# Linear attention and a gated MLP in one kernel: the output projection joined to the down products of two more token pairs, the gate and up products of three FF-tile pairs as seven products instead of eight, and three of four h sums moved to VectorE

## Chip, core and metric

One NeuronCore of one Trainium2 chip runs the whole program in one launch. The metric is the device time in microseconds (us). The kernel before took 211.93 us, the median of three runs (211.37 to 212.01). The execution that was profiled took 212.13 us.

## What is computed

The input x has 2048 tokens of 512 values. It is normalised once (xn), and two branches and the input itself are added.

```python
xn  = layernorm(x)
qkv = xn @ wqkv                              # 32 heads of 16
pq, pk = q @ w_phi, k @ w_phi                # per head
phi = concat(softmax(p), softmax(-p))        # of pq and of pk, 32 features
kv, z = phi_k^T v, sum(phi_k)                # over all tokens
o   = (phi_q kv) / (phi_q z + 1e-6)
out = x + o @ wo + ((xn @ w_gate) * (xn @ w_up)) @ w_down    # F = 1792
```

## The kernel before

**Tiles.** Tokens come in 16 tiles of 128, or 8 pairs of tiles p = 0 to 7. F is cut into 14 FF tiles of 128, taken as 7 pairs (tile ft with tile ft + 7). The model dimension of 512 is four blocks of 128.

**Who does what.** TensorE (PE) does all products into PSUM. ScalarE (ACT) takes exponentials and copies gate products (and snapshots of partial sums) out of PSUM. VectorE (DVE) multiplies gate by up into the array h (`hT`), adds the pieces of the seven-product schemes, sums the softmax denominators and divides. GpSimd (POOL) forms sums of weights and of h in SBUF. The queue of SyncE (SP) issues loads, transposing DMAs and stores.

**Seven products.** A 2 by 2 block product normally takes 8 block products. The kernel does many of them in Winograd's form with 7, which need sums of blocks made beforehand on either side, and additions behind. For the tokens 512 to 1535, and 6 of the 7 FF-tile pairs, gate and up are done so (`BLOCK`, with `WSUMS` for the weights on GpSimd and `XSUMS` for the tokens on VectorE). The down product of each token pair is done so too: `SSUMS(p)` makes four sums S3, S1, S2, S4 of h (128 by 896 float16 each) on GpSimd, `TSUMS` the sums of the weights, and the steps P1 to P7 do seven matmuls of 256 columns each.

**The output projection.** `CAT_STEPS(p)`, for the pairs in `CAT` (1 to 5), also puts the attention output through the same seven products: each P step gets two more matmuls (P1o to P7o), with sums `SOSUMS(p)` of the attention output and `TOSUMS` of wo on GpSimd. `DOWN_STEPS(p)`, for pairs 0, 6 and 7, adds wo in the plain way: 16 matmuls of 256 columns, four of them in the step W22.

**The last 512 tokens.** `U2(ft, s_lo)` does gate and up for one FF tile and 256 tokens: 8 matmuls of 256 columns, one ScalarE copy (`ge`) and one VectorE product (`h`). 28 such units are spread between the down steps by `some(fr)`, with `Q(t)` (query features) and `NUM(t)` (attention numerator, VectorE steps nd, nr, no).

**Order.** The program records steps in the order of the source; `_plan` then reorders them on each engine by its own costs, dependencies and priorities, and `_emit_all` writes each engine's list with semaphore waits. Each engine then runs its list strictly in that order: an instruction that waits holds up all behind it. A PSUM bank is reused in the order of recording, from a ring of banks; the down steps use two fixed banks. In `sums`, a sum placed on VectorE is marked `lock`, so that the planner lets it run only while GpSimd does nothing.

```python
e3, e1, e2, e4 = (DVE if c == "D" else POOL for c in SE.get(p, "PPPP"))
sums(e3, S3, A11, A21, ALU.subtract, f"S3.{p}", 0)
sums(e1, S1, A21, A22, ALU.add, f"S1.{p}", 0)
sums(e2, S2, S1, A11, ALU.subtract, f"S2.{p}", 0)
sums(e4, S4, A12, S2, ALU.subtract, f"S4.{p}", 0)
```

The helper lines that the profile names: L510 is every matmul but the warm-up, L463 every ScalarE operation, L781 every sum of blocks (S, So, To, Ts, weight sums, and the X sums on VectorE), L731 and L729 the feature scaling on GpSimd, L940 the product h of `U2`, L1071 the additions (`post`) behind the down products, L862 and L868 those of `BLOCK`, L722 the softmax sums, L999, L1001 and L1005 the division.

Of the kernel before, what the change touches and what calls it, by code (L numbers as in the profile page):

```python
# [16 lines left out]
D = 512  # L17
# [342 lines left out]
PD = -1  # L360
PX = -1
SE = {}
UE = 1.6
QP0 = 1
QP1 = 2
# [2 lines left out]
TRQ = 1500.0  # L368
TRO = 800.0
PS = -1  # L370
CAT = (1, 2, 3, 4, 5)
SOE = POOL
TOE = POOL
PLN = 0
# [12 lines left out]
def _build(nc, es, A_x, A_wqkv, A_w_phi, A_wo, B_w_gate, B_w_up, B_w_down, out):  # L387
# [65 lines left out]
    def bank(b, lo=0, n=512):  # L453
        return psum[:, b * 512 + lo: b * 512 + lo + n]
# [67 lines left out]
    def group(o, pairs):  # L522
        n = len(pairs)
        return [(o, l, r, i == 0, i == n - 1) for i, (l, r) in enumerate(pairs)]
# [15 lines left out]
    def xnT(q, s_lo, n):  # L540
        return xnT_v[:, q, s_lo:s_lo + n]
# [328 lines left out]
    def BLOCK(kind, ft, ba):  # L870
# [58 lines left out]
                act_op(gslot(ft, 2), pa, name=f"ge{ft}.2", prio=PA)  # L929
        return [p1, p7, p6, p2, p4, p5, p3]  # L930

    def U2(ft, s_lo):
        b = nb()
        mm(group(bank(b, 0, 256), [(wg_v[:, q, ft * 128:(ft + 1) * 128], xnT(q, s_lo, 256)) for q in range(NQ)])
           + group(bank(b, 256, 256), [(wu_v[:, q, ft * 128:(ft + 1) * 128], xnT(q, s_lo, 256)) for q in range(NQ)]),
           name=f"gu{ft}.{s_lo}")
        g = gring()[:, 0:256]
        act_op(g, bank(b, 0, 256), name=f"ge{ft}.{s_lo}")
        h = hT_v[:, ft, hs(s_lo):hs(s_lo) + 256]
        dve(lambda e: e.tensor_tensor(out=h, in0=bank(b, 256, 256), in1=g, op=ALU.mult), [bank(b, 256, 256), g], [h],  # L940
            name=f"h{ft}.{s_lo}")

    def GU2(fts, s_lo, bg, bu, order):
# [48 lines left out]
    def NUM(t):  # L992
        nv = numb()
        mm([(nv[:, c, 0:68], qT_v[:, t % NQT, c, :], kvbd_v[:, c, :], True, True) for c in range(8)], name=f"n{t}")
        sm = qsum_v[:, t % 5, :].rearrange("p (c h s) -> p c h s", c=8, s=2)[:, :, :, 0]
        w = qw_v[:, t % 4, :]
        wv4 = w.rearrange("p (c h) -> p c h", c=8)
        den = nv[:, :, 64:68]
        dve(lambda e: e.scalar_tensor_tensor(out=wv4, in0=sm, scalar=1e-6, in1=den, op0=ALU.mult, op1=ALU.add),  # L999
            [qsum_v[:, t % 5, :], den], [w], cost=210.0, name=f"nd{t}")  # L1000
        dve(lambda e: e.reciprocal(out=w, in_=w), [w], [w], cost=360.0, name=f"nr{t}")  # L1001
        o = oslot(t)
        ov = o.rearrange("p (c h d) -> p c h d", c=8, h=4)
        src = nv[:, :, 0:64].rearrange("p c (h d) -> p c h d", h=4)
        dve(lambda e: e.tensor_tensor(out=ov, in0=src, in1=wv4[:, :, :, None].to_broadcast([128, 8, 4, 16]),  # L1005
                                      op=ALU.mult), [src, w], [o], cost=600.0, name=f"no{t}")
        dst = oT_v[:, t % 4, :, :]
        sc.dma(SP, dst, o, 131072, turn=True, reads=[o], writes=[dst], name=f"oT{t}").reserve = TRO
# [17 lines left out]
    def hA(half, t):  # L1026
        s = hs(t * 128)
        return hT_v[:, half * HF:(half + 1) * HF, s:s + 128]

    def SSUMS(p):  # L1030
        assert ui[0] >= (10 if p < 2 else NA2 if p < 6 else NA2 + (14, 28)[p - 6])
        S1, S2, S3, S4 = (S_v[:, p % 2, w] for w in range(4))
        A11, A12, A21, A22 = hA(0, 2 * p), hA(1, 2 * p), hA(0, 2 * p + 1), hA(1, 2 * p + 1)
        e3, e1, e2, e4 = (DVE if c == "D" else POOL for c in SE.get(p, "PPPP"))
        sums(e3, S3, A11, A21, ALU.subtract, f"S3.{p}", 0)
        sums(e1, S1, A21, A22, ALU.add, f"S1.{p}", 0)
        sums(e2, S2, S1, A11, ALU.subtract, f"S2.{p}", 0)
        sums(e4, S4, A12, S2, ALU.subtract, f"S4.{p}", 0)

    To_v = sbv("x", 12 * 512, 4 * 512).bitcast(F16).rearrange("p (w k j) -> p w k j", w=4, k=2)  # L1040
    So_v = sbv("vext", 0, 2 * 4 * 256).bitcast(F16).rearrange("p (r w k s) -> p r w k s", r=2, w=4, k=2)
# [37 lines left out]
    def DOWN_STEPS(p):  # L1079
# [1 line left out]
        final = p == NT // 2 - 1  # L1081
        S1, S2, S3, S4 = (S_v[:, p % 2, w] for w in range(4))
        A11, A12, A22 = hA(0, t1), hA(1, t1), hA(1, t2)
        pa, pb = bank(4, 0, 256), bank(5, 0, 256)
        t11, t21, t22 = (tf_v[:, p % 2, w] for w in range(3))

        def o(t, c):
# [31 lines left out]
                store(t1, 256, 256)  # L1119

        def s7():
            d = bank(nb(), 0, 256) if final else pb
            mm(prod(d, A12, B21, True) + wo_part(d, t1, 0), name=f"P2.{p}")
            post(p, o(t1, 0), d, t11, "c11")
            store(t1, 0, 256 if p == NT // 2 - 1 else 512)
# [18 lines left out]
    def CAT_STEPS(p):  # L1144
# [2 lines left out]
        S1, S2, S3, S4 = (S_v[:, p % 2, w] for w in range(4))  # L1147
        O1, O2, O3, O4 = (So_v[:, p % 2, w] for w in range(4))
        R1, R2, R3, R4 = (To_v[:, w] for w in range(4))
        A11, A12, A22 = hA(0, t1), hA(1, t1), hA(1, t2)  # L1150
        pa, pb = bank(4, 0, 256), bank(5, 0, 256)
        t11, t21, t22 = (tf_v[:, p % 2, w] for w in range(3))

        def o(t, c):
# [2 lines left out]
        def x(t, c):  # L1157
            return x_res(t)[:, c * 256:(c + 1) * 256]
# [4 lines left out]

        def s1():
            P(1, pa, A11, B11, oA(0, t1), oB(0, 0), True, False)
            post(p, t11, pa, x(t1, 0), "t11")

        def s2():
            P(2, pb, A12, B21, oA(1, t1), oB(1, 0), True, True)
            post(p, o(t1, 0), pb, t11, "c11")  # L1170

        def s3():
            P(7, pb, S3, T3, O3, R3, True, False)
# [15 lines left out]
        def s7():  # L1189
            P(3, pa, S4, B22, O4, oB(1, 1), False, True)  # L1190
            post(p, o(t1, 1), pa, x(t1, 1), "c12")
            store(t1, 0, 512)
        return [s1, s2, s3, s4, s5, s6, s7, lambda: None]

    one = nc.const_aps.tensor(1.0, [128, 512], BF16)

# [48 lines left out]
    rest = [(U, f, sg) for ft in range(NB, NF // 2) for f in (ft, ft + NF // 2) for sg in (1, 2)]  # L1245
    units += rest
    NA2 = len(units)
    units += [(U2, ft, s_lo) for s_lo in (1536, 1792) for ft in range(NF)]
    ui = [0]

    def nextU():
        if ui[0] < len(units):
# [44 lines left out]
    assert ui[0] >= NA  # L1297
    load_x(SP, 4, 4, name="rx")
    load_x(SP, 8, 4, name="rx")
    down = DOWN_STEPS(0)  # L1300
    nextU()
    KVS(NT, 1)
    KVX()
    ring_banks[0] = [0, 1, 2, 3]
    rp[0] = 0
    nextU()
    down[0]()
    down[1]()
    NUM(0)
    nextU()  # L1310
    SSUMS(1)
    nextU()
    NUM(1)
    TOSUMS(TOE)
    u0 = ui[0]
    n_left = len(units) - u0
    NP = NT // 2
    for p in range(NP):
        def some(fr):
            k = int(round(u0 + n_left * min(1.0, (p + fr) / (NP - UE))))  # L1320
            while ui[0] < min(k, len(units)):
                nextU()
        a, b = 2 * p + 2, 2 * p + QA
        if p == 2:
            load_x(SP, 12, 4, name="rx", slot=0)
        def Qs(pos):
            for k, at in ((0, QP0), (1, QP1)):
                if at == pos and b + k < NT:
                    Q(b + k)
        if p > 0:  # L1330
            down = CAT_STEPS(p) if p in CAT else DOWN_STEPS(p)
            Qs(0)
            down[0]()
            some(0.1)
            Qs(1)
            down[1]()
        some(0.2)
        if a < NT:
            NUM(a)
        if p == 0:  # L1340
            Qs(0)
            Qs(1)
        Qs(2)
        down[2]()
        some(0.4)
        Qs(3)
        down[3]()
        if 2 <= p + 1 < NP:
            SSUMS(p + 1)
        if a + 1 < NT:  # L1350
            NUM(a + 1)
            if p + 1 in CAT:
                SOSUMS(p + 1, SOE)
        some(0.5)
        down[4]()
        some(0.65)
        Qs(5)
        down[5]()
        some(0.8)
        down[6]()  # L1360
        some(1.0)
        down[7]()

    assert ui[0] == len(units)
    sc.chain("P6.7 P2.7 P5.7 P4.7 P3.7")

    for st in sc.steps:
        if st.eng in (ACT, DVE, POOL) and not isinstance(st.lane, tuple) and st.idx > late[0]:
# [40 lines left out]
```

The softmax here doesn't subtract the row's maximum and nothing guards it: scores larger than these inputs give would overflow.

## Time and profile before

| | |
|---|---|
| median of three runs | 211.93 us |
| profiled execution, whole | 212.13 us |
| its span, first to last instruction | 209.8 us |
| PE busy | 204.5 us (97%), 1603 matmul records; 1620 weight loads |
| VectorE busy | 158.7 us (76%), 307 instructions |
| ScalarE busy | 113.3 us (54%), 293 instructions |
| GpSimd busy | 169.6 us (81%), 215 instructions |
| granted TensorE clock | 1.00 |

Busy is the time in which an engine has at least one instruction under way; on VectorE and ScalarE the records of neighbours overlap by some 0.1 us. A few matmul records are missing, no weight load is. In the view by windows, each row gives the length of the stretch and then, for PE, PEld (weight loads), DVE, ACT and POOL, the busy time with the number of instructions in brackets. In rows of the timeline the first number is the start in us from the span's start, the second the length. A row of the groups ends in busy us, mean ns of one, and the idle time of the engine before them.

### The profile page before, as it was taken

What the parts mean: (1) busy time and instruction counts of PE and PEld (TensorE: products, weight loads), DVE (VectorE), ACT (ScalarE), POOL (GpSimd) and SP (SyncE); (2) the same over time, 40 slices, a digit from 0 to 9 for tenths busy, and PEclk for the clock granted to TensorE, in tenths of its full rate; (3) what the DMA queues carried; (4) which work ended last, traced back from release to release, by engine and by line L of the source; (5) the groups of instructions that cost most, each with busy time, mean ns of one, the idle gap of its engine ahead of it and who ended that gap; (6) DMA issues with size and microseconds to landing.
All of it is one profiled execution on the core that took longest, in us unless ns stands there. A gap on an engine that the chain in (4) does not pass through costs nothing.

```text
span 209.8 us, 4274 instructions
## 1 busy us (share of the span) xinstructions
PE 204.5 (97%) x1603; PEld 136.3 (65%) x1620; DVE 158.7 (76%) x307; ACT 113.3 (54%) x293; POOL 169.6 (81%) x215
## 2 busy tenths in 40 slices
PE   8999999999999999999999999999999999999995
PEld 3875444444454444454456797988978888799884
DVE  4857799998966797989987875948659486695743
ACT  4756999698796959697822613416144251531000
POOL 4061698439999999999999999999999989990540
PEclk9999999999999999999999999999999999999999
DMA  5999924964100000222521135183351705635211
GB/s 161 334 264 355 245 59 96 327 137 140 32 18 0 3 0 0 50 52 53 197 54 28 25 78 125 34 174 101 70 129 25 175 13 115 80 75 128 50 52 50
DMA packets 50244, 21.52 MB, mean 103 GB/s; under 512 B 37424, under 2 KB 50224, under 8 KB 50224
## 3 DMA queue, kind: packets, MB, share of 16 engines
q1 hardware_dynamic: 49552, 20.93, 40.5%
q10 hardware_dynamic: 672, 0.33, 0.6%
q8 instruction: 12, 0.20, 0.4%
q14 instruction: 8, 0.07, 0.1%
HBM read 10.24 MB, written 2.10 MB: 59 GB/s over the span
## 4 chain that ended last, share of the span: by engine, by line
PE 80%; POOL 7%; ACT 5%; DMA 3%; DVE 2%; issue 1%; DVEq 0%
PE ps L510 78%; ACT arena L463 5%; POOL arena L781 4%; DMA arena<-arena 3%; PE ps L1199 2%; POOL arena L731 2%; POOL arena L636 1%; DVE arena L781 1%; DVE arena L722 1%; POOL arena L729 0%; DVE arena L756 0%; ACT ps L463 0%; DVE arena L940 0%; DVE arena L1071 0%; DVEq L349 0%
## 5 line engine op out<-in xcount | busy, mean ns | idle before, releaser
L510 PE MATMUL ps<-arena 128*128 128x256 bf16 (+5 forms) x1593 | 200.3, 286 | 1.9 <-ACT ps L463 0.4
L510 PEld LDWEIGHTS ps<-arena 128*128 128x128 bf16 (+1 forms) x1610 | 135.0, 98 | 67.8 <-ACT arena L463 2.0
L781 POOL TENSOR_TENSOR arena<-arena 128x256 f16<-128x256 bf16 (+3 forms) x120 | 124.3, 1060 | 12.9 <-DVE arena L940 7.4
L463 ACT ACTIVATE arena<-ps 128x512 bf16<-128x512 f32 (+3 forms) x168 | 83.4, 533 | 67.9 <-PE ps L510 64.7
L722 DVE TENSOR_REDUCE arena<-arena 128x64 f32<-128x1024 bf16 x32 | 38.6, 1208 | 1.0 <-ACT arena L463 0.9
L1071 DVE TENSOR_TENSOR arena<-ps,arena 128x256 bf16<-128x256 f32 (+1 forms) x56 | 23.3, 422 | 17.4 <-PE ps L510 16.1
L463 ACT ACTIVATE arena<-arena 128x64 f32<-128x64 f32 (+4 forms) x96 | 28.4, 314 | 12.2 <-DVE arena L722 8.8
L731 POOL TENSOR_TENSOR arena<-arena 128x512 bf16<-128x512 bf16 x32 | 33.8, 1060 | 0.4
L940 DVE TENSOR_TENSOR arena<-ps,arena 128x256 f16<-128x256 f32 x30 | 12.4, 420 | 11.3 <-ACT arena L463 9.7
L862 DVE TENSOR_TENSOR arena<-ps,arena 128x512 f16<-128x512 f32 x24 | 16.1, 683 | 1.0 <-PE ps L510 0.8
L811 DVE TENSOR_TENSOR arena<-ps,arena 128x512 f16<-128x512 f32 x14 | 9.5, 684 | 4.9 <-PE ps L510 3.5
L756 DVE TENSOR_TENSOR arena<-ps,arena 128x512 bf16<-128x512 f32 x16 | 10.8, 683 | 2.1 <-ACT arena L463 1.5
L627 DVE BATCH_NORM_STATS2 arena<-arena 128x6 f32<-128x512 bf16 x16 | 10.5, 673 | 2.1 <-DMA arena<-in_A_x_dram 2.0
L868 DVE TENSOR_TENSOR ps<-ps,arena 128x512 f32<-128x512 f32 x12 | 8.2, 696 | 4.3 <-PE ps L510 3.0
L1005 DVE TENSOR_TENSOR arena<-ps,arena 128x512 bf16<-128x512 f32 x16 | 11.0, 685 | 0.3
L729 POOL TENSOR_TENSOR arena<-arena 128x32 f32<-128x32 f32 x32 | 8.3, 262 | 3.5 <-ACT arena L463 3.4
L609 POOL TENSOR_TENSOR arena<-arena 128x128 bf16<-128x128 bf16 x4 | 1.6, 428 | 8.7 <-DMA arena<-in_A_w_phi_dram 8.7
L636 POOL TENSOR_SCALAR arena<-arena 128x1 f32<-128x1 f32 x12 | 3.3, 290 | 6.0 <-ACT arena L463 6.0
L868 DVE TENSOR_TENSOR arena<-ps,arena 128x512 bf16<-128x512 f32 x12 | 8.0, 680 | 0.0
L463 ACT ACTIVATE ps<-ps 128x512 f32<-128x512 f32 x12 | 7.2, 600 | 0.0
L1001 DVE RECIPROCAL arena<-arena 128x32 f32<-128x32 f32 x16 | 5.6, 352 | 0.5
L1199 PE MATMUL ps<-const-bfloat16-1.0 128*128 128x512 bf16 x10 | 4.4, 626 | 0.8 <-PEq L1394 0.8
(22 smaller groups left out, 26.6 us busy)
## 6 DMA issues: line engine op xcount, KB each, us to landing
arena<-in_A_x_dram SPq DMA_DIRECT2D x6, 512.0 KB, 5.2
arena<-in_B_w_down_dram SPq DMA_DIRECT2D x1, 1792.0 KB, 7.6
out_dram<-arena SPq DMA_DIRECT2D x14, 128.0 KB, 2.0
arena<-in_B_w_gate_dram SPq DMA_DIRECT2D x1, 768.0 KB, 7.9
arena<-in_B_w_up_dram SPq DMA_DIRECT2D x1, 768.0 KB, 8.4
arena<-arena SPq DMA_TRANSPOSE x44, 2.5
arena<-in_B_w_gate_dram SPq DMA_DIRECT2D x2, 256.0 KB, 4.4
arena<-in_B_w_gate_dram SPq DMA_DIRECT2D x1, 512.0 KB, 6.1
```

Source lines behind the costliest of these rows:

```text
L463: return e.activation(out=out_ap, in_=in_ap, func=func, scale=scale, **kw)
L510: ins = e.matmul(o, lhsT=l, rhs=r, start=s, stop=p, skip_group_check=True)
L627: dve(lambda e, t=t: e.bn_stats(stats_v[:, t, :], x_tile(t)), [x_tile(t)], [stats_v[:, t, :]], cost=600.0, name=f"st{t}", win=win, prio=prio)
L722: dve(lambda e, ei=ei, so=so: e.tensor_reduce(out=so, in_=ei.rearrange("p (h f) -> p h f", f=16), axis=AX.X, op=ALU.add), [ei], [so], cost ...
L731: pool(lambda e: e.tensor_tensor(out=ev[:, :, 1, :], in0=ev[:, :, 1, :], in1=ratio[:, :, None].to_broadcast([128, H, 16]), op=ALU.mult), [ ...
L756: dve(lambda e: e.tensor_tensor(out=o1, in0=src, in1=rp_[:, :, :, None].to_broadcast([128, 8, 4, 16]), op=ALU.mult), [src, rs_v[:, t % 4, ...
L781: fn = lambda e: e.tensor_tensor(out=out_, in0=a_, in1=b_, op=op)
L862: dve(lambda e: e.tensor_tensor(out=h, in0=src, in1=g, op=ALU.mult), [src, g], [h], name=f"h{ft}.{sg}", prio=PD)
L868: dve(lambda e: e.tensor_tensor(out=o, in0=src, in1=sn, op=ALU.add), [src, sn], [o], name=name, prio=PD)
L940: dve(lambda e: e.tensor_tensor(out=h, in0=bank(b, 256, 256), in1=g, op=ALU.mult), [bank(b, 256, 256), g], [h], name=f"h{ft}.{s_lo}")
L1005: dve(lambda e: e.tensor_tensor(out=ov, in0=src, in1=wv4[:, :, :, None].to_broadcast([128, 8, 4, 16]), op=ALU.mult), [src, w], [o], cost=6 ...
L1071: dve(lambda e: e.tensor_tensor(out=out_, in0=in_ps, in1=in_sb, op=ALU.add), [in_ps, in_sb], [out_], cost=328.0, name=f"{name}.{p}")
```

## The change

Three things are changed in the program, and the planner makes a new order from it.

- `CAT` becomes (0, 1, 2, 3, 4, 5, 6): pairs 0 and 6 use `CAT_STEPS`, with `SOSUMS` on GpSimd for both.
- For FF-tile pairs 0, 1 and 2 (`NX = 3`) and the last 512 tokens, 12 of the 28 units `U2` are replaced by six `ZBLOCK`s (gate and up of each pair), each of 7 products of two matmuls of 256 columns. `ZXSUMS` (four sums of 128 by 512) and six `ZWSUMS` (four sums of 128 by 256 each) are recorded on GpSimd. Each `ZBLOCK` takes three of the four ring banks.
- `SED = 'PDDD'`: of the four h sums of each pair, S3 stays on GpSimd, and S1, S2 and S4 go to VectorE.

Also: the last pair's two fixed banks become 2 and 3, `U2` swaps the halves of its bank for the last tokens, and units are paced by a weight. The other new constants are left at values that change nothing.

```diff
-CAT = (1, 2, 3, 4, 5)
+CAT = (0, 1, 2, 3, 4, 5, 6)
+SED = 'PDDD'
+AB = {7: (2, 3)}
+NX = 3
+WSE = POOL
+XSE = POOL
...
+    def ZXSUMS():
+        X1, X2, X3, X4 = (Tz_v[:, w] for w in range(4))
+        for n, (o_, a_, b_) in enumerate(((X1, zB(0, 1), zB(0, 0)), (X3, zB(1, 1), zB(0, 1)), (X2, zB(1, 1), X1),
+                                          (X4, zB(1, 0), X2))):
+            sums(XSE, o_, a_, b_, ALU.subtract, f"Xz{n}", 0)
...
+        sums(WSE, S3, A(0, 0), A(1, 0), ALU.subtract, f"{kind}z3.{ft}", 0)
+        sums(WSE, S1, A(1, 0), A(1, 1), ALU.add, f"{kind}z1.{ft}", 0)
+        sums(WSE, S2, S1, A(0, 0), ALU.subtract, f"{kind}z2.{ft}", 0)
+        sums(WSE, S4, A(0, 1), S2, ALU.subtract, f"{kind}z4.{ft}", 0)
...
+    def ZBLOCK(kind, ft):
...
+        def p1():
+            pa = take("a")
+            xprod(pa, A(0, 0), zB(0, 0), True, "b1" + nm)
+            seed(take("c"), pa, "sd" + nm)
+        def p7():
+            pb = take("b")
+            xprod(pb, S(2), X3, True, "b7" + nm)
+            st["p7"] = zsnap()
+            act_op(st["p7"], pb, name="s7" + nm, prio=PB)
+        def p2():
+            xprod(st["c"], A(0, 1), zB(1, 0), False, "b2" + nm)
+            done(ft, 0, st["c"])
+            free("c")
+        def p6():
+            xprod(st["a"], S(1), X2, False, "b6" + nm)
+            st["u2"] = zsnap()
+            act_op(st["u2"], st["a"], name="s2" + nm, prio=PB)
+        def p4():
+            pb = st["b"]
+            xprod(pb, A(1, 1), X4, False, "b4" + nm)
+            if kind == "g":
+                zadd(zgslot(ft2, 0), pb, st["u2"], "a4")
+            else:
+                zadd(pb, pb, st["u2"], "a4")
+                done(ft2, 0, pb)
+            free("b")
+        def p5():
+            xprod(st["a"], S(0), X1, False, "b5" + nm)
+            if kind == "g":
+                zadd(zgslot(ft2, 1), st["a"], st["p7"], "a5")
+            else:
+                pt = bank(nb(), 0, 256)
+                zadd(pt, st["a"], st["p7"], "a5")
+                done(ft2, 1, pt)
+        def p3():
+            xprod(st["a"], S(3), zB(1, 1), False, "b3" + nm)
+            done(ft, 1, st["a"])
+            free("a")
+        return [p1, p7, p2, p6, p4, p5, p3]
...
-        e3, e1, e2, e4 = (DVE if c == "D" else POOL for c in SE.get(p, "PPPP"))
...
+        es = [DVE if c == "D" else POOL for c in SE.get(p, SED)]
...
-    units += [(U2, ft, s_lo) for s_lo in (1536, 1792) for ft in range(NF)]
+    std = [ft for ft in range(NF) if ft % (NF // 2) >= NX]
+    units += [(U2, ft, 1536) for ft in std]
+    blocks = [(kind, ft) for ft in range(NX) for kind in "gu"]
+    for i, b in enumerate(blocks):
+        units += [(f,) for f in ZBLOCK(*b)]
+        if i + 3 < len(blocks):
+            units.append((ZWSUMS,) + blocks[i + 3])
+    NA3 = len(units)
+    units += [(U2, ft, 1792) for ft in std]
```

`xprod` is two matmuls, `seed` and `act_op` one ScalarE operation, `zadd` one VectorE addition, and `done` is a ScalarE copy for gate and a VectorE product for up.

## The prediction, made before the changed kernel ran

> **What bounds the kernel now.** I read the page first, then the chain of waits in order of time, the groups by shape, and the busy time by windows.
>
> ```profile
> PE 204.5 (97%) x1603; PEld 136.3 (65%) x1620; DVE 158.7 (76%) x307; ACT 113.3 (54%) x293; POOL 169.6 (81%) x215
> ```
>
> ```profile
> 53.87 0.25 POOL arena L636
> ...
> 54.15 2.48 ACT arena L463 x4
> 56.63 0.50 ACT ps L463
> 57.13 0.05 issue
> 57.17 2.60 PE ps L510 x24
> ...
> 179.27 27.60 PE ps L510 x267
> ```
>
> In the chain, from 57.17 us to 206.87 us every piece is PE or a gap of 0.05 us: no other engine is late in that time. Just before, at 57.17, PE waits for ScalarE, and ScalarE for GpSimd.
>
> ```profile
> 200.80:206.20 5.40, 5.40 (x52) 4.84 (x50) 2.55 (x6) 0.00 (x0) 1.09 (x1) 1.00 0.18 61
> 46.00:57.00 11.00, 10.42 (x54) 4.46 (x53) 9.97 (x17) 9.15 (x25) 10.61 (x17) 1.00 0.42 104
> 57.00:72.00 15.00, 14.72 (x106) 7.72 (x109) 10.49 (x15) 12.75 (x31) 15.00 (x22) 1.00 0.05 10
> 72.00:108.00 36.00, 35.79 (x212) 16.94 (x215) 33.43 (x46) 26.56 (x70) 36.00 (x48) 1.00 0.25 59
> 136.00:170.00 34.00, 33.84 (x316) 28.32 (x317) 22.27 (x49) 11.58 (x30) 33.76 (x32) 1.00 0.46 106
> ```
>
> The first row holds matmuls of 256 columns alone: 50 weight loads in 5.40 us, 0.108 us for each matmul, full clock (1.00) and no holes. So the end is set by the number of matmuls. The other rows show what is near it: VectorE is busy 93% of 72 to 108, but only 66% of 136 to 170. GpSimd is full, but nothing after 57 waits for it.
>
> The Trainium skill (Perfetto Trace Analysis, Identifying the Most-Contended Engine, and the skill's first page) says not to take PE's busy share for closeness to the limit, but the weight loads' share; that is 65% here and would leave a third of the time free. The spacing of 0.108 us decides against that reading: matmuls stand without holes.
>
> **The change, part by part.**
>
> ```profile
> L781 POOL TENSOR_TENSOR arena<-arena 128x896 f16<-128x896 f16 x32 | 60.1, 1883 | 11.3 <-DVE arena L940 7.4 <-DMA arena<-arena 3.4 <-PE ps L510 0.2
> L463 ACT ACTIVATE arena<-ps 128x256 bf16<-128x256 f32 x38 | 14.0, 383 | 40.4 <-PE ps L510 39.7 <-DVE arena L940 0.5
> L940 DVE TENSOR_TENSOR arena<-ps,arena 128x256 f16<-128x256 f32 x30 | 12.4, 420 | 11.3 <-ACT arena L463 9.7 <-PE ps L510 1.2
> ```
>
> *PE.* Joining wo takes 2 matmuls from pair 0 and 2 from pair 6 (65 to 63 each). The six blocks do 6 x 7 x 2 = 84 matmuls in place of 12 x 8 = 96. In all 16 fewer, of 256 columns each: 16 x 0.108 = **1.73 us less**, all on the path. The built order agrees (1620 to 1604 matmuls, no other size touched).
>
> *GpSimd.* It loses 24 h sums, 24 x 1.88 = 45.1 us. It gains 24 sums of gate and up weights (0.67 each, as the 256-wide row of its line has it: 16.1), four sums of tokens (1.16: 4.6) and eight for wo (0.67: 5.4): 26.1. Net 19 us less, of no worth after 57 us, since no one waits for it there. Its cover: the new weight sums stand on its queue some 10 us ahead of the products. If they came late, each would cost PE up to 0.67 us.
>
> *The wait at 57 us.* In the weight loads of that stretch PE stands idle for 0.89 us, for a ScalarE copy queued behind the normalisation of tiles 14 and 15, which waited for GpSimd. There S1.0 (1.88 us) leaves GpSimd's queue, but a weight sum of 1.16 us moves ahead, and the VectorE sum will hold GpSimd for some half a microsecond. So the wait stays; but the order now puts kv4 (8 small matmuls, about 0.3 us) into it. I take **0.3 us less**; bounds 0 and 0.9.
>
> *ScalarE.* Per block 3 copies more, and gate's copies fall from 4 to 2: 24 copies in place of 12, 12 x 0.38 = 4.6 us. It is busy 11.58 of 34 us there: nothing, if its order is right; a copy that is waited for costs 0.2 us from the end of its product to its start, 0.38, and 0.05 to the next product, so 0.63 us of other matmuls must stand between.
>
> *VectorE.* This is the disputed part. 24 h sums come to it, 12 more products and additions of 256 columns (24 in place of 12), and 2 final additions go. How long is an h sum? The nearest rows are the X sums, the same operation over 512 values:
>
> ```profile
> 39.49 0.74 DVE L781 TENSOR_TENSOR arena<-arena 128x512 f16<-128x512 bf16 x2
> 41.95 1.33 DVE L781 TENSOR_TENSOR arena<-arena 128x512 f16<-128x512 bf16 x2
> 42.15 0.85 POOL L781 TENSOR_TENSOR arena<-arena 128x256 f16<-128x256 bf16 x1
> ```
>
> Undisturbed, two take 0.74 with 0.41 for one: one each 0.33 us. For 896 values at most 0.33 x 896/512 = 0.58; I take 0.55. Beside GpSimd, two took 1.33 and GpSimd's own sum 0.85 in place of 0.67: the two shut each other out, about 0.3 us per VectorE sum here. The bounds of a wait are 0 and 1.88, one whole GpSimd sum; I take 0.45: half of an operation of 0.9 us, between the 1.05 of now (33.76 us over 32 in 136 to 170) and the 0.67 of the sums that come.
>
> The Trainium skill (SBUF — State Buffer, Who interferes with whom) has an exclusive lock on a shared port pair, the loser blocked for the whole instruction. That speaks against this change: with 0.9 us of wait per sum in place of 0.45, the stretch below would come out about 3 us longer.
>
> Now stage by stage. *46 to 72 us:* five h sums (S1.0, S2.0, S4.0, S1.1, S2.1), 5 x (0.55 + 0.45) = 5.0 us, go onto VectorE. Its idle time there is 11 - 9.97 + 15 - 10.49 = 5.5 us, so they just fit. But queues are in order: S2.0 waits for the transposes of tiles 14 and 15, which SP issues from 54.99 on and which land about 2.5 us after issue; behind S2.0 are the additions that free PSUM banks for b7u.2 and b3u.1. S4.0 waits for the fold of wq. Going down VectorE's list against PE's with these lengths, PE waits about 0.45 us for the bank of vs7. I take **0.5 us more**; bounds 0 and 2.
>
> *72 to 108 us:* no h sum is placed there but S4.1 at its end; nothing.
>
> *The stretch of the six blocks,* PE from b2zg.0 to b3zu.2: 249 matmuls of 256 columns, 20 of 512 and six numerators, 249 x 0.108 + 20 x 0.216 + 6 x 0.34 = 33.3 us. VectorE's list for it has 70 operations: 6 softmax sums at 1.12 (spacing, a little under the length), 5 divisions at 1.0, 18 additions and 24 products or additions of the blocks at 0.335, 7 h sums at 0.55: 6.7 + 5.0 + 14.1 + 3.9 = 29.7 us, and 7 x 0.45 = 3.2 of waits: 32.9. It fits by a hair. Most covers in PE's order are 0.76 us or more (seven matmuls), as in the kernel before, where 0.87 us between P3o and the next P1 was enough without a wait. Two are 0.43: b3zu.1 to b1zg.2 over a VectorE product (needs 0.67) and b7zg.2 to b4zg.2 over a copy (0.63). That is 0.24 us once, as both fall together; **0.4 us more** with a second such place; bounds 0.2 and 4.
>
> *The end.* VectorE makes the last pair's sums in 0.55 us in place of 1.88, but these now stand among c22.6 and the division of tile 15, whose transpose P4.7 needs. Between n15 and P4.7 are 7.5 us of matmuls; the division, its queue and the transpose need 6 to 7. P3.6 waits for c22.6, up to 0.5. I take **0.1 us more**. SP's queue has the same 83 entries; two stores and the transposes of pair 0 change places, with transposes that PE wants several us later: nothing.
>
> **Sum.** -1.73 - 0.3 + 0.5 + 0.4 + 0.1 = -1.0 us. The profiled execution goes from 212.1 to 211.1; the median stands 0.2 below it, so **210.9 us**, 0.5% faster. About 0.3% (0.64 us) is what a measurement here can tell from no change.
>
> **Rivals.**
>
> *The plan holds without waits.* For it: PE's order is nearly without short covers. Then -1.73 - 0.3 to -0.9: 209.3 to 209.9.
>
> *The products go and waits take their place.* Each of the six blocks is a chain of seven short products with a copy or addition between them, in three of four ring banks. If each block costs 0.3 us of waits (one 0.63 us need over a 0.33 cover), 6 x 0.3 = 1.8 us eat the matmuls: 211.9. For it: the order has little to put between them, as `U2` units wait behind the blocks. Against it: down products and Q's stand between most.
>
> *Slower: VectorE becomes the bound in the block stretch.* The mechanism is the shared exclusion of VectorE's h sums and GpSimd. It decides from the wait at which 29.7 + 7w exceeds 33.3, w = 0.51 us; at w = 0.9 it is 2.7 us over, and the five early sums cost 5 x 0.45 = 2.2 more, of which half may be caught up. 212.1 - 1.0 + 2.7 + 1.1 = 214.9 at worst, 213 in the middle. For it: GpSimd stays some 85% busy there. Against it: only 7 sums stand there, and VectorE's list has work that nobody waits for soon (softmax sums, h sums of the next pair).
>
> **Chances.** Forecast 0.50 (its own range 210.2 to 211.5), no waits 0.13, waits eat the gain 0.15, VectorE bound 0.22. From these: faster by over 0.3% 0.58, within 0.3% 0.19, slower 0.23. The range 209.6 to 213.4 leaves out about a tenth on each side.
>
> **What would show it.** In the changed profile: PE still 0.108 us per 256-column matmul; the block stretch 33.3 to 34 us long; VectorE above 90% busy in it; L781 on VectorE 24 times at 0.6 to 1.1 us, and GpSimd's operations beside them lengthened by up to 0.5. The forecast is wrong if PE waits for VectorE come to over 2 us in the waits list, if the h sums on VectorE take over 1.2 us on average, or if the piece around 57 us grows.

## The result, and the profile after

The changed kernel takes **222.57 us** (median of six runs, 221.81 to 223.38), where the kernel before took 211.97 us in the runs beside it. The ratio is 1.0509 (95% interval 1.0478 to 1.0541): 5% slower, where 0.5% faster was forecast, and 9 us above the top of the range. The profiled execution took 222.71 us, with a span of 221.0 us where it was 209.8.

The line numbers have moved. `sums`, L781 before, is L795 here; every matmul (L510) is L524; the product h of the first 1536 tokens (L811) is L825; the softmax sums (L722) are L736; the feature scaling (L731) is L745. In the kernels with an edited order below, `sums` is L823 or L824.

From the page, the busy line that was shown of before, and the granted clock in 40 slices of 5.5 us (tenths of the full clock, 9 for 90% or more):

```profile
PE 206.9 (94%) x1604; PEld 134.4 (61%) x1604; DVE 187.7 (85%) x341; ACT 117.8 (53%) x305; POOL 155.2 (70%) x227
...
PEclk9999999999999999999985799999999999999999
```

1604 weight loads: the 16 matmuls are gone, as the forecast had it. VectorE is busy 29 us longer, of which 24 h sums at the forecast 1.0 us and 12 more additions would be 28. So the page by itself looks like the forecast. The clock line has a dent in slices 21 to 23 of 40.

The chain of waits in order of time, where before every piece from 57.17 to 206.87 us was PE or a gap of 0.05 us:

```profile
46.81 53.83 PE ps L524 x326
...
107.81 2.64 DVE arena L795
110.46 9.01 issue
119.46 0.69 DVE arena L825
120.15 0.05 issue
120.20 97.87 PE ps L524 x902
```

The chain no longer breaks at 57 us, the stretch of the blocks is inside the last piece, unbroken, and in between there is one new thing: an h sum on VectorE (L795), with 9 us in which nothing seems to go on. (The pieces left out, from 100.64 to 107.81, are ScalarE and VectorE operations that lead up to that sum.) The list of waits has it from TensorE's side:

```profile
PEld ps L524 <- DVE arena L825: 10.3, 1, 10.3
PE ps L524 <- DVE arena L825: 10.2, 1, 10.2
```

One wait, once, of 10.3 us. The rows of the timeline at that place, VectorE's and then GpSimd's (start, length, operation; a row of x10 is ten operations one behind the other, with the shape of the first):

```profile
107.13 0.68 DVE L770 TENSOR_TENSOR arena<-ps,arena 128x512 bf16<-128x512 f32 x1
107.73 11.81 DVE L795 TENSOR_TENSOR arena<-arena 128x896 f16<-128x896 f16 x1
119.46 1.28 DVE L825 TENSOR_TENSOR arena<-ps,arena 128x512 f16<-128x512 f32 x2
```

```profile
107.64 1.06 POOL L745 TENSOR_TENSOR arena<-arena 128x512 bf16<-128x512 bf16 x1
108.65 10.41 POOL L795 TENSOR_TENSOR arena<-arena 128x512 f16<-128x512 bf16 x10
```

The h sum S4.1 is 11.81 us long instead of 0.6 to 1.5. GpSimd ran kp15 and ten sums (To2, S3.1, To3, Xz0, Xz1, Xz2, gz3.0, Xz3, gz1.0, uz3.0) meanwhile, up to 119.06; then it had to wait for ScalarE, and S4.1 ended 0.48 us later. Behind S4.1 in VectorE's list stood h6.1, h6.2 and kvx. h6.1 and h6.2 free the banks that TensorE needs next, so TensorE stood from the end of kv15 (its last weight load ends at 109.89) to 120.20. Windows around the hole (the columns as before: length, PE, PEld, DVE, ACT, POOL, clock):

```profile
107.70:109.40 1.70, 1.70 (x10) 0.75 (x9) 1.70 (x2) 0.46 (x1) 1.70 (x2) 1.00 0.00 0
109.40:120.20 10.80, 0.62 (x10) 0.38 (x9) 10.80 (x3) 0.73 (x2) 9.66 (x10) 0.73 0.00 0
120.20:125.00 4.80, 4.80 (x19) 2.05 (x20) 2.40 (x5) 0.60 (x1) 0.00 (x0) 0.53 0.00 0
```

VectorE "busy" for 10.80 of 10.80 us is VectorE waiting: an instruction under way counts as busy whether it moves data or not. After the hole TensorE ran at a granted clock of 0.53 for 4.8 us; four steps there (u13.1, g13.2, n0, u13.2) took 2.0 us longer than their matmuls do at 1.00.

The sum of the changes of the span, from the starts of the weight loads: 16 matmuls less, -1.7; the hole, +10.4; the low clock behind it, +2.0; which leaves +0.5 for all else of the +11.2 measured (221.0 - 209.8).

The other h sums are as forecast, as the group shows when the one is taken out:

```profile
L795 DVE TENSOR_TENSOR arena<-arena 128x896 f16<-128x896 f16 x24 | 30.5, 1271 | 1.8 <-PE ps L524 1.5 <-DMA arena<-arena 0.2
```

(30.5 - 11.8) / 23 = 0.81 us each. None of the others waited for more than the one GpSimd operation that was running.

### The profile page after: what moved, and what is told of

The parts are those of the page before. It is cut to its first block, busy times and chain, and to the rows that moved or that the text cites. A ratio compares the mean times of both kernels' runs of the same rounds, so it can differ in the third digit from the quotient of the medians.

```text
span 221.0 us, 4305 instructions
## 1 busy us (share of the span) xinstructions
PE 206.9 (94%) x1604; PEld 134.4 (61%) x1604; DVE 187.7 (85%) x341; ACT 117.8 (53%) x305; POOL 155.2 (70%) x227
## 4 chain that ended last, share of the span: by engine, by line
PE 89%; issue 5%; DVE 4%; ACT 1%; DVEq 0%
PE ps L524 87%; PE ps L1345 2%; DVE arena L795 1%; ACT arena L477 1%; DVE arena L876 1%; DVE ps L882 1%; DVE arena L770 0%; DVE arena L825 0%; DVE arena L882 0%; DVE arena L736 0%; DVE arena L1203 0%; DVEq L349 0%; DVE arena L1266 0%; DVEq L322 0%
## 5 line engine op out<-in xcount | busy, mean ns | idle before, releaser
L524 PE MATMUL ps<-arena 128*128 128x512 bf16 (+5 forms) x1594 | 202.7, 289 | 10.7 <-DVE arena L825 10.2
L524 PEld LDWEIGHTS ps<-arena 128*128 128x128 bf16 (+1 forms) x1594 | 133.1, 98 | 80.9 <-DVE arena L825 10.3
L477 ACT ACTIVATE arena<-ps 128x512 bf16<-128x512 f32 (+4 forms) x174 | 84.6, 528 | 70.9 <-PE ps L524 69.1
L795 POOL TENSOR_TENSOR arena<-arena 128x256 f16<-128x256 bf16 (+3 forms) x132 | 108.9, 848 | 10.4 <-DMA arena<-arena 6.1
L736 DVE TENSOR_REDUCE arena<-arena 128x64 f32<-128x1024 bf16 x32 | 38.7, 1208 | 1.5 <-ACT arena L477 1.5
L795 DVE TENSOR_TENSOR arena<-arena 128x896 f16<-128x896 f16 (+1 forms) x32 | 34.4, 1086 | 2.1 <-PE ps L524 1.5
L745 POOL TENSOR_TENSOR arena<-arena 128x512 bf16<-128x512 bf16 x32 | 33.9, 1061 | 0.4
L743 POOL TENSOR_TENSOR arena<-arena 128x32 f32<-128x32 f32 x32 | 9.2, 288 | 22.8 <-ACT arena L477 22.5
L825 DVE TENSOR_TENSOR arena<-ps,arena 128x512 f16<-128x512 f32 x14 | 9.4, 683 | 4.7 <-PE ps L524 3.2
L477 ACT ACTIVATE ps<-ps 128x512 f32<-128x512 f32 (+1 forms) x18 | 9.4, 523 | 2.2 <-PE ps L524 2.1
L1069 DVE TENSOR_TENSOR arena<-ps,arena 128x256 f16<-128x256 f32 x18 | 7.4, 417 | 2.9 <-ACT arena L477 2.9
```

The lines of the kernel that those rows point to most:

```text
L477: return e.activation(out=out_ap, in_=in_ap, func=func, scale=scale, **kw)
L524: ins = e.matmul(o, lhsT=l, rhs=r, start=s, stop=p, skip_group_check=True)
L736: dve(lambda e, ei=ei, so=so: e.tensor_reduce(out=so, in_=ei.rearrange("p (h f) -> p h f", f=16), axis=AX.X, op=ALU.add), [ei], [so], cost ...
L745: pool(lambda e: e.tensor_tensor(out=ev[:, :, 1, :], in0=ev[:, :, 1, :], in1=ratio[:, :, None].to_broadcast([128, H, 16]), op=ALU.mult), [ ...
L795: fn = lambda e: e.tensor_tensor(out=out_, in0=a_, in1=b_, op=op)
L825: dve(lambda e: e.tensor_tensor(out=h, in0=bank(bu), in1=g, op=ALU.mult), [bank(bu), g], [h], name=f"h{ft}.{sg}")
```

## The experiments

The question was not whether S4.1 cost the time but why this sum of 24 was shut out, as others met GpSimd running back to back too and got in at the next boundary between two operations.

**Is it GpSimd, and its having no pause?** Four runs. First, S4.1 moved to GpSimd behind S3.1, all else in the same order:

```diff
+    st = by_name["S4.1"]
+    sc.by_eng[DVE].remove(st)
+    st.eng = st.lane = POOL
+    sc.by_eng[POOL].insert(sc.by_eng[POOL].index(by_name["S3.1"]) + 1, st)
```

> The order of the changed kernel, with one instruction moved: S4.1 goes from VectorE to GpSimd, right behind S3.1. Theory (GpSimd's unbroken run of ten operations shuts out that one VectorE sum): the 10.6 us hole in PE at kv15 and the slow clock behind it go; 222.6 - 10.6 - 2 = 210 us, and GpSimd's four sums longer queue costs nothing. Rival (the seven-product blocks and the joined wo wait for their sums on GpSimd): no more than the hole's clock share changes, 219 us or above, as GpSimd gets 1.9 us more. Rival (VectorE has too much work in all): 1 us less.

Measured: 211.85 us, ratio 1.0004 (0.9973 to 1.0034). The hole is gone. The median is 1.9 us above the expectation, the one profiled execution (211.06) 1.1. Part of that has a name: GpSimd is now later by a whole sum, and TensorE waits for it between 118 and 126 us:

```profile
PEld ps L553 <- POOL arena L824: 0.8, 2, 0.6
```

Second, every GpSimd operation behind kp15 waits for the end of the one before it, which leaves a gap of 0.08 us between them:

```diff
+    lst = sc.by_eng[POOL]
+    for a, b in zip(lst[lst.index(by_name["kp15"]):], lst[lst.index(by_name["kp15"]) + 1:]):
+        if a not in b.deps:
+            b.deps.append(a)
```

> The changed kernel's order, unchanged; from kp15 on, each GpSimd operation waits for the one before it to be complete. Theory, in the form that VectorE gets in only when GpSimd's pipeline is empty for a moment: S4.1 takes at most the rest of kp15 and 0.6 us, 1.6 us in all, and the time is about 210.5 us. Rival (a VectorE sum waits for something else that ends at 119 us, or for all that GpSimd has been given): S4.1 stays at 11 us or more, and the time at 222 us or above, as GpSimd gets slower by some 0.08 us per operation.

Measured: 216.7 us, ratio 1.0218 (1.0145 to 1.0291). On the sum the expectation held:

```profile
107.90 1.45 DVE L824 TENSOR_TENSOR arena<-arena 128x896 f16<-128x896 f16 x1
```

On the total it missed by 6 us: with gaps everywhere GpSimd falls behind, and TensorE waits for its sums later on (the longest wait, 3.5 us, ends at 161.3 us).

Third, the seven-product blocks left out (`NX = 0`), so that GpSimd has fewer sums behind kp15:

> The seven-product blocks of the last 512 tokens are undone (all 28 plain units, no sums for them); wo joined for pairs 0 to 6 and three h sums of four on VectorE stay, and the planner orders anew. GpSimd's run behind kp15 is then three operations (To2, S3.1, To3) up to one that waits for ScalarE. Theory (shut out until GpSimd pauses): S4.1 takes 1.0 + 4.1 + 0.5 = 5.5 us, PE loses some 4.5 us at kv15, and the time is 211.9 - 0.4 + 4.5 = 216 us. Rival (the blocks are what is slow): 211 us. Rival (VectorE has too much work): as before or 1 us above.

Measured: 216.73 us, ratio 1.0216 (1.0162 to 1.027). GpSimd's run ends at 112.67, and S4.1 ends 0.49 us later:

```profile
107.73 5.43 DVE L795 TENSOR_TENSOR arena<-arena 128x896 f16<-128x896 f16 x1
```

So in the kernel the sum lasts until GpSimd's run ends, with ten operations left or three; and a gap of 0.08 us is enough of an end.

Fourth, the two engines alone. GpSimd does six to twelve operations back to back, of one kind or mixed, and one VectorE h sum asks up to 0.9 us into the first:

> The disputed wait by itself; all of the reference's computation is left out (x is copied to the output). In 30 trials GpSimd runs 6 to 12 sums in a row, and VectorE, after a sum over 128 to 1024 values as a delay, makes one h sum (896 float16). Kinds of row: 896-wide, 512-wide, 256-wide, the mixture of the changed kernel, the feature scaling, and 512-wide where each waits for the one before. Theory (shut out for the whole run): the VectorE sum ends 0.5 us after GpSimd's last of the row, 4 to 11 us, in all kinds but the last, and there after one operation. Rival (one operation at most): all 0.6 to 2.5 us. If only some kinds shut it out, the kind decides, and the table shows which.

No sum took over 2.12 us: none of the 30 missed a boundary between two GpSimd operations. So the theory in this form fell: GpSimd without a pause was not the whole condition.

**Is it the moment at which the sum asks?** A finer sweep of the moment with the two engines alone, 397 sums:

> The kernel's work is left out but for x copied to out; its time says nothing. 397 trials of a back-to-back GpSimd run (six 512-column differences; eight of 256 columns; a feature scaling, two 512, an 896-column h sum and four 512) with one VectorE h sum of 896 columns arriving at a time that is moved in steps of 4 ns to 19 ns through the first GpSimd operation. Theory A (whether VectorE gets in at a boundary hangs on where its request falls; once it has lost it goes on losing as long as GpSimd has no pause): between 1 in 20 and 1 in 4 of the sums take the whole rest of the run (4 us and more instead of 0.6 to 1.8), in neighbouring steps. Theory B (back-to-back operations alone never shut VectorE out for more than the one in progress; something else of the kernel, such as its other engines, does): none of the 397 takes more than 1.8 us.

```profile
L92 DVE TENSOR_TENSOR arena<-arena 128x896 f16<-128x896 f16 x397 | 405.5, 1022 | 0.0
```

The longest took 1.6 us; eleven that asked at most 0.04 us after an operation had begun waited for the whole of it, and none for more. Theory A fell here, and again in the kernel, where a memset was put ahead of S4.1 (`e.memset(sc.tiny, 0.0)` before it is issued):

> The changed kernel with one instruction more: a memset of one element on VectorE just ahead of S4.1, so that S4.1 asks some 0.06 us later. All else in the same order. Theory A (whether VectorE gets in at GpSimd's boundaries hangs on the phase of its request, and stays lost once lost): S4.1 takes at most 1.9 us, the hole before kv15 is gone, about 211 to 212 us. Theory B (S4.1 is shut out for as long as GpSimd runs without a pause, wherever in an operation it asks): S4.1 again takes 11.5 to 11.9 us, about 222.5 us.

Measured: 222.69 us, ratio 1.0518 (1.0465 to 1.0572).

```profile
108.42 11.80 DVE L824 TENSOR_TENSOR arena<-arena 128x896 f16<-128x896 f16 x1
108.45 0.06 DVE L349 MEMSET arena<- 128x1 f32 x1
```

**Is it the place in the order?** S4.1 left on VectorE but moved behind no1 (`lst.insert(lst.index(by_name["no1"]) + 1, ...)`):

> The changed kernel with S4.1, still on VectorE, moved 11 steps back in VectorE's order: behind no1, so that h6.1, h6.2 and kvx run ahead of it and GpSimd's run up to uz3.0 is over, or nearly, when it asks. Theory B (shut out while GpSimd runs without a pause; what costs time is what queues behind it): S4.1 takes under 2 us, the hole before kv15 is gone, 210 to 212 us. Rival (VectorE has too much to do between 107 and 135 us, whatever the order): still over 215 us.

Measured: 211.99 us, ratio 1.0016 (0.9991 to 1.004). h6.1, h6.2 and kvx now run ahead, so the hole is gone. But S4.1 was again shut out, past two boundaries, until GpSimd's run ended at 119.65; it took longer than the 2 us expected, and TensorE stood 1.7 us for an addition (L1231) that is queued behind it:

```profile
117.61 2.52 DVE L823 TENSOR_TENSOR arena<-arena 128x896 f16<-128x896 f16 x1
PEld ps L552 <- DVE arena L1231: 1.7, 1, 1.7
```

Two parts of the change were then taken by themselves. The changed kernel with all h sums back on GpSimd (`SED = 'PPPP'`):

> The changed kernel without its third part: all four h sums of a pair on GpSimd as before; wo joined for pairs 0 to 6 and the 7-product blocks kept. The plan orders it anew. If the h sums on VectorE were the only loss: 210 to 211.5 us. Rival (GpSimd, with 28 sums more for the blocks and all h sums, is now late): its sums hold up TensorE between 120 and 180 us, 213 us or more.

Measured: 224.53 us, ratio 1.0609 (1.0563 to 1.0655). The rival won: without the move to VectorE the blocks' sums make GpSimd late, and TensorE waits for it from 140 us on.

```profile
PE 206.5 (93%) x1584; PEld 133.0 (60%) x1604; DVE 162.8 (73%) x317; ACT 117.6 (53%) x305; POOL 193.5 (87%) x251
...
POOL 47%; PE 46%; issue 3%; ACT 2%; DVE 1%; DVEq 0%
```

Half of the chain is now GpSimd. The second part of the change needs the third. And the first part alone (`SED = 'PPPP'`, `NX = 0`):

> The first part of the change alone: wo joined to down for pairs 0 to 6, no blocks, all h sums on GpSimd. TensorE's work stays the same; the prediction gave this part no time but at the wait of 57 us and the end: 211.3 to 212.3 us. Rival (what the changed kernel lost beyond the hole comes from joining): 213 us or more.

Measured: 211.08 us, ratio 0.9972 (0.9944 to 1.0001), at the edge of what can be told. It is a little better than expected, and TensorE's work does not stay the same, as the expectation had it: 1616 weight loads in place of 1620, the four matmuls (0.43 us) that the prediction had counted for this part.

**Is it the length of the run?** Now the sums of six kernels were set side by side: how many GpSimd operations had gone by without a pause since VectorE last got in, when the sum asked. Up to 13 operations every sum got in at the next boundary; those that missed a boundary had asked after 51 (S4.1), 59 (S4.1 moved back) and 72 (S1.2 of the run with S4.1 on GpSimd, which missed one). Alone on the chip, with runs of 50 or 88 operations and the sum asking later and later:

> The kernel's work is left out but for x copied to out; its time says nothing. GpSimd runs 50 differences of 512 columns (or 88 of 256, or 50 that each count up a semaphore and wait for the one before the last) back to back, some 55 us, and VectorE asks for one h sum after 0.5 to 48 us of it; at the end, one run with eleven sums, one each 4 us. Theory C (a GpSimd run that has gone on long enough without a pause no longer lets VectorE in; in the kernels seen so far every sum that asked within 21.3 us of the last pause got in at the next boundary, and the three that asked 38 us or more after it did not): sums that ask up to 20 us take under 1.9 us, those from 40 us on take until the run ends, 8 to 16 us. Theory D (the length of the run has no part in it): all take under 1.9 us.

The VectorE sums of five successive trials, asking 12, 16, 20, 24 and 28 us into a run of some 55.5 us:

```profile
189.16 0.82 DVE L107 TENSOR_TENSOR arena<-arena 128x896 f16<-128x896 f16 x1
249.21 1.25 DVE L107 TENSOR_TENSOR arena<-arena 128x896 f16<-128x896 f16 x1
309.32 35.93 DVE L107 TENSOR_TENSOR arena<-arena 128x896 f16<-128x896 f16 x1
369.57 31.91 DVE L107 TENSOR_TENSOR arena<-arena 128x896 f16<-128x896 f16 x1
429.87 27.86 DVE L107 TENSOR_TENSOR arena<-arena 128x896 f16<-128x896 f16 x1
```

This is the lock-out, with nothing else of the kernel there: up to 16 us a sum gets in, from 20 us on it is shut out. In the runs of 50 operations that lasts to the end of the run, up to 35.93 us and 31 boundaries. With the semaphore counts and waits on GpSimd it is the same (35.93 us at 20). In the three late trials with 88 operations of 256 columns it ended sooner, though GpSimd made no pause: the sums got in ahead of the 80th, the 81st and the 82nd operation, 5.5, 4.9 and 4.3 us before the runs ended (850.51, 906.27 and 962.05):

```profile
814.97 30.01 DVE L107 TENSOR_TENSOR arena<-arena 128x896 f16<-128x896 f16 x1
882.79 18.58 DVE L107 TENSOR_TENSOR arena<-arena 128x896 f16<-128x896 f16 x1
950.68 7.10 DVE L107 TENSOR_TENSOR arena<-arena 128x896 f16<-128x896 f16 x1
```

So the end of the run is the longest that a sum was shut out, not always how long. In the last trial, with a sum each 4 us, all eleven got in, the last one 52 us into the run.

In the kernel, one gap of 0.08 us was put 12 us ahead of S4.1, by letting Ts3.0 wait for qp2:

```diff
+    lst = sc.by_eng[POOL]
+    st = by_name["Ts3.0"]
+    st.deps.append(lst[lst.index(st) - 1])
```

> The changed kernel with one wait more, and nothing moved: GpSimd's Ts3.0, 12 us ahead of S4.1, waits for the end of qp2, the operation just before it on GpSimd, so that GpSimd's run of 62 operations is cut by a gap of some 0.1 us. Theory C: S4.1 asks 12 us into the run, gets in at the end of kp15 and takes 1.5 us instead of 11.8; the hole before kv15 is gone; 210.5 to 212 us. Theory D (something that lies at 107 to 120 us shuts VectorE out, not the run's length): S4.1 again 11.5 us or more, 222.5 us.

Measured: five runs of 222.29 to 223.47 us and one of 210.40. In the profiled one (222.56) S4.1 was shut out:

```profile
108.15 11.91 DVE L823 TENSOR_TENSOR arena<-arena 128x896 f16<-128x896 f16 x1
```

So the gap does not simply undo it; the run of 210.40 was not profiled, and that S4.1 got in there is inferred from its time. What a gap and a sum that gets in do was then measured alone:

> The kernel's work is left out but for x copied to out; its time says nothing. GpSimd runs 32 or 50 differences of 512 columns (1.11 us each) in 44 trials: 17 without a pause, in which VectorE's one h sum asks 16 to 20 us in, in steps of 0.25 us; 16 in which one operation, 22 us in, waits for the one before it (a gap of 0.08 us) and the sum asks 1.5 to 14 us behind that gap; 4 with four such gaps in a row; 7 in which a first sum asks after 10 us (and gets in) and a second 8 to 28 us behind that one. Theory C (a GpSimd run without a pause is what shuts VectorE out; a gap of 0.08 us ends the run): the sums behind a gap get in at the next boundary; of the seven second sums those that ask over 20 us after the run's start are shut out. Theory V (what counts is the time since VectorE last held what the two share, or since GpSimd last stood still for longer; a short gap ends nothing unless VectorE asks just then): one threshold between 16 and 20 us; the sums behind a gap, 24 us and more into the run, are shut out to the run's end, the 12 of them that ask 2 us or more behind it at least; of the seven second sums those up to 14 or 16 us behind the first get in, those 22 and 28 us behind do not.

Four trials with one gap at 22.3 us, the sum asking 2.2, 6.3, 10.4 and 14.5 us behind it:

```profile
651.06 0.62 DVE L109 TENSOR_TENSOR arena<-arena 128x896 f16<-128x896 f16 x1
711.45 0.85 DVE L109 TENSOR_TENSOR arena<-arena 128x896 f16<-128x896 f16 x1
771.71 1.23 DVE L109 TENSOR_TENSOR arena<-arena 128x896 f16<-128x896 f16 x1
832.03 19.25 DVE L109 TENSOR_TENSOR arena<-arena 128x896 f16<-128x896 f16 x1
```

Theory V, that a short gap ends nothing, fell: the gap starts the count anew. So does a sum that gets in: second sums that asked 8.2, 12.3 and 14.3 us behind the end of the first got in, those 16.4 us and more behind it did not. Both thresholds lie at 13 to 15 operations of 1.11 us, and the S4.1 with the gap 12 us ahead of it asked in the 14th operation behind that gap. (Behind the last of four gaps in a row, a sum that asked 14.9 us after it, in the 14th operation too, got in.) That pointed to a count of operations, which three lengths of operation can tell from time:

> The kernel's work is left out but for x copied to out; its time says nothing. GpSimd runs differences of 256 columns (0.63 us each), of 512 (1.11 us) or h sums of 896 (1.84 us) back to back; VectorE's one h sum asks in the n-th of them, n from 6 to 30 (256 columns) or 6 to 20, each twice. Theory N (operations are counted: some 14 of them without a pause shut VectorE out): the threshold lies at the same n, 13 to 15, for all three lengths: at 8 to 9.5, 14.5 to 16.5 and 24 to 28 us. Theory T (time is counted): it lies at the same time, 14 to 17 us, for all three: n of 23 to 27, 13 to 15 and 8 or 9.

For operations of 256, 512 and 896 columns, the last sum that got in and the first that did not:

```profile
245.91 0.89 DVE L107 TENSOR_TENSOR arena<-arena 128x896 f16<-128x896 f16 x1
264.16 8.95 DVE L107 TENSOR_TENSOR arena<-arena 128x896 f16<-128x896 f16 x1
...
1430.51 1.00 DVE L107 TENSOR_TENSOR arena<-arena 128x896 f16<-128x896 f16 x1
1461.10 15.39 DVE L107 TENSOR_TENSOR arena<-arena 128x896 f16<-128x896 f16 x1
...
2644.55 1.12 DVE L107 TENSOR_TENSOR arena<-arena 128x896 f16<-128x896 f16 x1
2696.61 24.86 DVE L107 TENSOR_TENSOR arena<-arena 128x896 f16<-128x896 f16 x1
```

They asked at 8.4 and 9.1 us, at 15.0 and 15.0 us, and at 25.1 and 27.0 us into the run: three different times, one count. Of the 110 sums, every one that asked in one of the first 13 operations got in, five of the six that asked in the 14th did, and of those that asked in the 15th or later none did. (In the trials of 50 operations above, the sum at 249.21, which asked 15.9 us into its run, stood in the 15th and got in; the edge is not quite sharp.) Theory N held, theory T fell.

**Does keeping the count short in the kernel bring the gain?** Once with S4.1 where it was, and GpSimd's To0 waiting for kq14, 3.5 us ahead of S4.1:

```diff
+    lst = sc.by_eng[POOL]
+    st = by_name["To0"]
+    st.deps.append(lst[lst.index(st) - 1])
```

> The changed kernel with one wait more, and nothing moved: GpSimd's To0 waits for the end of kq14 just before it, which makes a gap of some 0.08 us 3.5 us and 5 operations ahead of S4.1's request. Theories N and T alike: S4.1 gets in at the end of kp15 and takes 1.5 us in every run; the hole is gone; 210 to 211 us, below the kernel before. Rival (the gap does not reach the kernel's S4.1, as the gap 12 us ahead did not in 5 runs of 6): 222.5 us in most runs.

Measured: **210.53 us** (twelve runs, 210.19 to 211.42), ratio to the kernel before 0.9937 (0.9911 to 0.9962). One wait, which leaves a gap of 0.08 us on an engine that nobody waits for there, makes the changed kernel 12 us faster:

```profile
107.72 1.50 DVE L823 TENSOR_TENSOR arena<-arena 128x896 f16<-128x896 f16 x1
109.15 1.28 DVE L853 TENSOR_TENSOR arena<-ps,arena 128x512 f16<-128x512 f32 x2
```

And once without the wait, S4.1 moved behind t11.0, where GpSimd stands still:

> The changed kernel with S4.1, still on VectorE, behind t11.0, 13 steps later than it was and two later than in the run that put it behind no1: it should ask after 120 us, when GpSimd stands still for qq4. All theories of the lock-out: S4.1 takes 0.6 to 1.1 us, the wait of 1.6 us at gu5.1536 is gone, 210 to 211.2 us. Rival (that wait came of something else than S4.1): still 211.7 us or more.

Measured: 210.59 us (ten runs, 210.06 to 211.23), ratio 0.9937 (0.9904 to 0.9969); S4.1 takes 0.62 us, and the wait of 1.7 us in the run with no1 is gone, so it had come of S4.1. These two versions beat both kernels; between them nothing can be told.

## Why the prediction was wrong, point by point

**The step that failed** is one line: "72 to 108 us: no h sum is placed there but S4.1 at its end; nothing." That one sum cost 12.4 us: 10.4 of waiting and 2.0 of the low clock behind it. Behind the line stood the bound in the VectorE part: "The bounds of a wait are 0 and 1.88, one whole GpSimd sum". The runs show that a wait has no such bound. With 13 operations or fewer it holds, and in the rows that I took the length from the sums asked in the first operation behind a pause or behind another sum; S4.1 asked after 51. The trace of before could not show it. Its only sums on VectorE, the X sums, end at 43 us, and the run in which GpSimd is busy 100% (36.00 of 36.00 us in 72 to 108, in my own rows) held no VectorE sum at all. That full GpSimd row was the warning: I read it as "GpSimd is full, but nothing after 57 waits for it", and did not ask who would have to get in beside it. Nor did the plan hold a place free: `lock` keeps kp15 back until S4.1 is over in the plan's own times alone, `_emit_all` writes no wait for it, and on the chip kp15 had begun (107.64) when S4.1 asked (107.73).

**What follows a wait was also missed.** I had costed S4.1 as one instruction. Behind it in VectorE's list stand h6.1 and h6.2, whose banks TensorE needs some 2 us after S4.1 asks. The rival "slower" had the right mechanism, the shared exclusion, and its chance of 0.22; but it looked for it in the block stretch, in seven waits of 0.9 us, and its worst added 3.8 us to the forecast. The place was another one, and the price over three times as high. Two of the signs named for a wrong forecast came: TensorE's waits for VectorE are over 2 us (10.3 in one), and the h sums on VectorE average 1.27 us, over 1.2.

**What held**, read from the version with the gap at To0, where this one event is taken out:

```profile
46.00:57.00 11.00, 10.64 (x55) 4.32 (x55) 10.97 (x18) 9.50 (x26) 10.62 (x17) 1.00 0.42 104
57.00:72.00 15.00, 14.89 (x108) 7.72 (x109) 13.68 (x20) 12.51 (x31) 13.94 (x21) 1.00 0.04 9
72.00:108.00 36.00, 35.73 (x212) 16.93 (x214) 32.53 (x45) 26.98 (x69) 35.92 (x48) 1.00 0.25 60
139.40:172.90 33.50, 33.34 (x316) 26.96 (x317) 31.64 (x69) 15.42 (x43) 29.29 (x37) 1.00 0.37 88
```

- *PE, -1.73:* 1604 weight loads, full clock; held.
- *46 to 72 us, -0.3 and +0.5:* TensorE is idle for 0.36 + 0.11 = 0.47 us, where it was 0.58 + 0.28 = 0.86: 0.4 less, where the two terms make 0.2 more. They differ in kind too. The wait for ScalarE at 57, which was to stay and be 0.3 shorter, is gone; in its place the weight loads wait three times for additions on VectorE, which is full there (10.97 of 11.00). The wait for the bank of vs7 came, with 0.3 us in place of 0.45 (the weight loads of v8, at 67.7). Between 52 and 58 us, before and then with the gap at To0:

```profile
PEld ps L510 <- ACT ps L463: 0.9, 1, 0.9
...
PEld ps L552 <- DVE arena L910: 0.5, 1, 0.5
PEld ps L552 <- DVE ps L910: 0.5, 1, 0.5
PEld ps L552 <- DVE arena L904: 0.4, 1, 0.4
```

- *72 to 108 us, with S4.1 let in:* 0.27 us idle, before 0.21; then "nothing" is right.
- *The block stretch, 33.3 + 0.4:* b2zg.0 at 139.40 to b3zu.2's end at 172.94, 33.5 us. VectorE is busy 94%, above the 90% named.
- *An h sum on VectorE, 0.55 + 0.45:* 0.61 to 0.62 alone, 0.84 with the waits on average in that version (20.1 us over 24).
- *The sum:* 210.9 forecast for the whole; 210.53 and 210.59 measured without the lock-out. With this one event taken out the sum holds to 0.4 us, although the two terms for 46 to 72 us did not come as forecast.

The Trainium skill's rule that was weighed (SBUF — State Buffer, Who interferes with whom), an exclusive lock with the loser blocked for the whole instruction, agrees with the sums up to 13 operations, and the trace bears out that it speaks against this change. The page also says that the order of issue decides who blocks. By the starts in the trace S4.1 asked before each of the ten operations behind kp15 and lost to all of them, so there the measurement decides against it.

## What to carry to other kernels

Where VectorE and GpSimd both work on SBUF operands, do not cost a VectorE sum by its length and one neighbour: count the GpSimd operations since its last pause or since VectorE last got in, and from about the 14th on take up to the whole rest of GpSimd's run as the wait, with all that is queued behind the sum. A single GpSimd operation that waits for the one before it, a few operations ahead of the sum, is enough to let it in, and costs 0.08 us; the same wait at every operation costs GpSimd's lead. An engine that is full and that nobody waits for is not harmless to a neighbour that shares something with it, and a busy VectorE may be a waiting one.

## What the hardware did that was not expected

- GpSimd's back-to-back operations let a two-input VectorE sum in at the next boundary for the first 13, and shut it out from about the 15th on: in the kernels and in most trials until GpSimd paused (11.81 us in the kernel, up to 35.93 us alone), in three trials until some 80 operations had run without a pause. The count is of operations: 9, 15 and 27 us for three lengths of them. A gap of 0.08 us or a sum that got in starts it anew. What in the chip counts is not shown by any run here, nor why the 14th and 15th go either way, nor what let the three in.
- Near that count the time of a kernel is not stable: with the gap 14 operations ahead, five runs took 222.3 to 223.5 us and one 210.4.
- VectorE's operations with one operand in PSUM (0.68 us for 512 columns, as in the rows above) ran beside the same GpSimd run without any such wait.
- A hole of 10.4 us on TensorE was followed by 4.8 us at a granted clock of 0.53, worth 2.0 us more.
